# Requesting only k of the third batch ahead of the first expert's w1, with another order for slots 4 to 6

## Chip, cores and metric

One core of a Trainium2 chip. The metric is the device time of one execution in microseconds (us). "Span" is the profiled execution without its fixed start and end, some 1.8 us less than the time. One execution of each kernel is traced; times are medians of several. In the traces PE is TensorE (matmuls), ACT ScalarE, DVE VectorE, POOL GpSimd; PEld is PE's loading of weights; L580 is line 580 of the kernel.

## The reference

Sliding-window attention (8 batches, 8 heads, 576 positions, head size 64; heads 0 to 3 a plain window of 32, heads 4 to 7 a window of 32 steps dilated by 4), then one expert of eight per batch, chosen by the mean of the attention output:

```python
scores = scale * q @ k.T ; scores = where(mask[h], scores, -1e9)
x      = softmax(scores) @ v                       # -> (8, 576, 512)
e      = argmax(x.mean(axis=1) @ w_gate, axis=1)   # one expert per batch
out[b] = gate_w[b] * (relu(x[b] @ w1[e[b]]) @ w2[e[b]])
```

The expert of a batch is known only after all its attention. So w1 (512 x 1024) and w2 (1024 x 512) of a batch can't be requested before that.

## The kernel before

Attention runs in slots, four per batch (two heads each). A slot is: scores (S), exp on ACT (X), mask on VectorE (M), products with v and with ones (A, B), Ln (K, L) and exp (R) for the reciprocal, normalisation (N). Ahead of it k and q are transposed on PE (T) and evacuated by VectorE (D) or ACT (A). Slots 0 to 6 follow a hand-written plan; from slot 7 on a loop mixes slots of batch b+2 with the FFN pieces of batch b. All loads of q, k, v, w1 and w2 are issued by POOL on one queue and cast from fp32 to bf16 on the way.

```python
load_qa(1); load_va(1); load_qb(1); load_vb(1)   # batch 1
load_qa(2)            # k and q of batch 2, heads 4 to 7: 288 KB each
load_va(2)            # its v, 256 KB, and v tail, 64 KB
# ...
def emit_gate(b):
    # gate matmuls on PE, max and index search on VectorE ...
    e_val = nc.values_load(mi[0:1, 0:1].bitcast(I32), engines=[ET.Pool], ...)   # L517
    nc.gpsimd.dma_start(out=w1b[:, 2:4, :], in_=moe_w1[ds(e_val, 1), ...])      # L521, 512 KB
    for a in range(2):
        nc.gpsimd.dma_start(out=w1b[half(a), 0:2, :], in_=moe_w1[...])          # L526, 256 KB each
    if b == 0:
        load_qb(2)            # k and q of heads 0 to 3
        load_w2(e_val, w2b)   # 1024 KB
        load_qa(3); load_vb(2)
    # ... else branch and the loads of batch b + 3
```

In the plan, `T1dk` is the transposes of batch 1's k of heads 4 to 7, `T1dk0D` the evacuation of their first bank (a part of the memory that PE writes to) by VectorE, `C1k` a copy that pairs the heads 0 to 3, `G0` the gate of batch 0, and `F` the first FFN piece: four matmuls of line L580, each reading a different quarter of w1.

The softmax here doesn't subtract the row's maximum and nothing guards it: scores larger than these inputs give would overflow.

## Time and profile before

| | before |
|---|---|
| time, median of 4 runs | 213.13 us (212.65 to 213.38) |
| span of the profiled execution | 210.6 us |
| PE busy | 92% |
| index search of the first gate ends | 23.98 us |
| last piece of the first w1 lands | 34.90 us |
| first FFN matmul (L580) | 35.04 us |

### The profile page before, as it was taken

The numbers are of one execution on the slowest core, as the hardware profiler recorded it, in microseconds if no ns is written. First come the engines' busy times: TensorE is split into PE (matmuls) and PEld (weight loads), VectorE is DVE, ScalarE is ACT, GpSimd is POOL, SyncE is SP. The second block draws the span as 40 slices with busy tenths as digits, with TensorE's granted clock in tenths as the row PEclk, the third lists the DMA queues.
The fourth block names the chain that finished last, engine by engine and source line by source line (L and its number), as shares of the span: only waits on it lengthen the run. The fifth ranks groups of instructions, "written<-read, shape, count | busy, mean of one in ns | idle before, by whom it ended". The sixth has DMA issues, their size and how long they took to land.

```text
span 210.6 us, 7428 instructions
## 1 busy us (share of the span) xinstructions
PE 192.7 (92%) x3130; PEld 140.5 (67%) x3145; DVE 129.2 (61%) x359; ACT 135.7 (64%) x270; POOL 82.5 (39%) x130
## 2 busy tenths in 40 slices
PE   5786775989989999999999999999999999999991
PEld 1565654877658965886578856895588558749741
DVE  5567764686587757775677666875777455325312
ACT  2487695677658876789658865886588656332320
POOL 7977585157460747045442556055104000500000
PEclk9755585899999999999999999999999999999998
DMA  5999999999999999999999999999995993499223
GB/s 73 184 176 193 185 197 210 213 180 202 197 219 246 226 205 195 248 241 209 186 245 251 214 198 250 239 226 210 241 244 98 212 217 134 79 210 230 107 113 111
DMA packets 46416, 41.12 MB, mean 195 GB/s; under 512 B 24880, under 2 KB 34096, under 8 KB 46384
## 3 DMA queue, kind: packets, MB, share of 16 engines
q0 software_dynamic: 38784, 31.20, 96.0%
q1 hardware_dynamic: 7600, 9.46, 13.8%
q8 instruction: 24, 0.39, 0.7%
q14 instruction: 8, 0.07, 0.1%
HBM read 62.41 MB, written 9.44 MB: 341 GB/s over the span
## 4 chain that ended last, share of the span: by engine, by line
PE 79%; DMA 11%; POOL 4%; issue 2%; DVE 1%; ACT 1%; POOLq 0%
PE m L580 31%; PE m L598 26%; PE n L349 8%; PE m L263 7%; DMA qm<-in_q_dram 4%; DMA w1b<-in_moe_w_dram 4%; PE m L613 3%; DMA vm<-in_v_dram 3%; PE ps L284 3%; PE m L510 1%; POOL vm L133 1%; POOL km L118 1%; POOL qm L121 1%; POOL vt L141 0%; ACT qk L271 0%
## 5 line engine op out<-in xcount | busy, mean ns | idle before, releaser
L580 PE MATMUL m<-xt,w1b 128*128 128x288 bf16 x512 | 67.0, 289 | 1.7 <-DMA w1b<-in_moe_w_dram 1.5
L580 PEld LDWEIGHTS <-w1b 128*128 128x128 bf16 x512 | 56.9, 114 | 7.9 <-issue 2.2
L598 PE MATMUL m<-w2b,ht 128*128 128x512 bf16 x241 | 56.9, 379 | 0.9 <-issue 0.2
L583 ACT ACTIVATE ht<-m 128x288 bf16<-128x288 f32 x77 | 31.6, 411 | 21.5 <-PE m L580 17.7
L598 PEld LDWEIGHTS <-ht 128*128 128x128 bf16 x256 | 24.1, 98 | 27.5
L487 DVE SCALAR_TENSOR_TENSOR xt<-n,rd 128x320 bf16<-128x320 f32 (+1 forms) x58 | 29.4, 544 | 11.2 <-ACT rd L460 10.3
L324 DVE TENSOR_TENSOR pt<-pt,mk 128x896 bf16<-128x896 bf16 x32 | 20.0, 625 | 22.1 <-ACT pt L317 22.1
L271 ACT ACTIVATE qk<-m 128x512 bf16<-128x512 bf16 (+1 forms) x28 | 20.8, 742 | 15.6 <-PE m L263 15.2
L317 ACT ACTIVATE pt<-ps 128x896 bf16<-128x896 f32 x32 | 29.0, 906 | 1.4 <-PE ps L284 1.4
L521 POOL DMA_DIRECT2D w1b<-in_moe_w_dram x8 | 5.7, 716 | 61.1 <-PE n L349 32.9
L131 POOL DMA_DIRECT2D vm<-in_v_dram x32 | 24.2, 772 | 10.2 <-DMA w1b<-in_moe_w_dram 3.0
L268 DVE COPY qk<-m 128x640 bf16<-128x640 bf16 (+1 forms) x28 | 22.3, 797 | 6.6 <-PE m L263 6.6
L585 DVE TENSOR_SCALAR ht<-m 128x288 bf16<-128x288 f32 x51 | 22.6, 455 | 4.7 <-PE m L580 3.8
L605 DVE TENSOR_SCALAR osb<-m,gbc 128x512 f32<-128x512 f32 x16 | 12.0, 747 | 17.7 <-PE m L598 17.7
L460 ACT ACTIVATE rd<-lnd 128x576 f32<-128x576 f32 x32 | 21.9, 684 | 1.0
L455 ACT ACTIVATE lnd<-n 128x256 f32<-128x256 f32 (+1 forms) x58 | 20.6, 406 | 1.7 <-PE n L349 1.6
L349 PEld LDWEIGHTS <-vm 64*64 64x64 bf16 x896 | 14.8, 114 | 9.2 <-SPq L410 2.8
L349 PE MATMUL n<-pt,vm 64*64 64x64 bf16 (+2 forms) x816 | 19.0, 198 | 1.6 <-DVE pt L324 1.2
L349 PE MATMUL n<-pt,ones 64*64 64x128 bf16 (+3 forms) x262 | 17.4, 251 | 0.0
L603 ACT ACTIVATE osb<-m,gbc 128x512 f32<-128x512 f32 x16 | 10.9, 682 | 8.7 <-PE m L598 8.7
L284 PEld LDWEIGHTS <-qk 64*64 64x64 bf16 x608 | 14.2, 116 | 2.8 <-issue 1.7
L284 PE MATMUL ps<-qk 64*64 64x96 bf16 (+3 forms) x608 | 14.8, 211 | 1.3 <-ACT pt L317 1.1
(72 smaller groups left out, 196.3 us busy)
## 6 DMA issues: line engine op xcount, KB each, us to landing
w2b<-in_moe_w_dram POOLq DMA_DIRECT2D x8, 1024.0 KB, 11.1
out_dram<-osb SPq DMA_DIRECT2D x32, 256.0 KB, 6.7
km<-in_k_dram POOLq DMA_DIRECT2D x16, 288.0 KB, 10.9
qm<-in_q_dram POOLq DMA_DIRECT2D x16, 288.0 KB, 11.3
w1b<-in_moe_w_dram POOLq DMA_DIRECT2D x8, 512.0 KB, 7.4
w1b<-in_moe_w_dram POOLq DMA_DIRECT2D x16, 256.0 KB, 8.3
vm<-in_v_dram POOLq DMA_DIRECT2D x8, 256.0 KB, 9.9
vm<-in_v_dram POOLq DMA_DIRECT2D x32, 64.0 KB, 7.9
```

Source lines behind the costliest of these rows:

```text
L131: nc.gpsimd.dma_start(out=t[:, h], in_=v[b, h, 0:512, :].rearrange("(c p) d -> p c d", p=P))
L268: nc.vector.tensor_copy(out=ev[x][0], in_=ev[x][1])
L271: nc.scalar.activation(out=ev[x][0], in_=ev[x][1], func=AF.Copy)
L284: nc.tensor.matmul(ps[half(e), a, o : o + rhs.free_size()], lhsT=lhsT, rhs=rhs, start=True, stop=True, skip_group_check=True)
L317: nc.scalar.activation(out=pt[:], in_=s["ps"][:, :, 0:NP], func=AF.Exp, scale=0.125)
L349: x = nc.tensor.matmul(oo, lhsT=lhsT, rhs=rhs, start=start, stop=True, skip_group_check=True)
L460: nc.scalar.activation(out=rd[:], in_=s["lnd", n][:], func=AF.Exp, scale=-1.0)
L487: nc.vector.scalar_tensor_tensor(out=o, in0=a0, scalar=1.0, in1=a1, op0=ALU.mult, op1=ALU.mult, accum_out=s["pool"][:, w, c : c + 1],)
L580: nc.tensor.matmul(hm, lhsT=w[:, fc % 4, :], rhs=s["xt"][:, c, cols], start=(c == 0), stop=(c == 3))
L583: nc.scalar.activation(out=o, in_=hm, func=AF.Relu)
L585: nc.vector.tensor_scalar_max(out=o, in0=hm, scalar1=0.0)
L598: nc.tensor.matmul(om, lhsT=s["ht"][:, fc, r * P : (r + 1) * P], rhs=s["w2"][:, fc, :], start=(fc == 0), stop=(fc == 7))
```

## The change

Intent: less should stand ahead of w1 in the load queue, and slots 4 to 6 should end earlier, so that the first FFN matmul starts earlier.

```diff
-    load_qa(2)
-    load_va(2)
+    load_tiles(2)
+    load_1(2, GO[0], "k")
@@ emit_gate, b == 0, after the three w1 requests
+            load_1(2, GO[0], "q")
+            load_va(2)
             load_qb(2)
             load_w2(e_val, w2b)
@@ plan, slots 4 to 6
-  ... T1dk L3 C1k R3 T1dk0A
-  N3 G0 T1dq T1dk1D T1dq0A T1pk T1dq1D C1q T1pk0A S4 T1pk1D T1pq X4 M4 S5 T1pq1D T1pq0A A4 X5 B4 K4 M5 L4 S6 R4
-  A5 X6 B5 K5 L5 N4 S7 M6 R5 A6 X7 N5 B6 K6 L6 M7 F R6 ...
+  ... T1dk L3 T1dk0D R3
+  T1dk1A N3 T1dq T1dq0A C1k G0 T1dq1A T1pk C1q S4 T1pk0D X4 T1pk1D T1pq T1pq0A S5 M4 T1pq1D X5 A4 K4 B4 L4 S6 M5 R4
+  A5 X6 B5 K5 L5 N4 S7 M6 R5 A6 X7 N5 B6 K6 L6 F M7 R6 ...
```

More of the change, by code (lines that the diff above doesn't have):

```diff
@@ L692 @@
         T0dk:7 MB T0dk0D T0dk1A T0dq D2 T0dq0A T0dq1D S0 C0k X0 T0pk M0 S1 T0pk1A C0q X1 T0pk0D T0pq T0pq0A M1 A0 T0pq1D
-        B0 K0 S2 L0 R0 A1 X2 N0 B1 K1 S3 L1 M2 R1 A2 X3 N1 B2 K2 L2 M3 R2 A3 N2 B3 K3 T1dk L3 C1k R3 T1dk0A
-        N3 G0 T1dq T1dk1D T1dq0A T1pk T1dq1D C1q T1pk0A S4 T1pk1D T1pq X4 M4 S5 T1pq1D T1pq0A A4 X5 B4 K4 M5 L4 S6 R4
-        A5 X6 B5 K5 L5 N4 S7 M6 R5 A6 X7 N5 B6 K6 L6 M7 F R6 T2dk T2dk0D T2dk1A N6
+        B0 K0 S2 L0 R0 A1 X2 N0 B1 K1 S3 L1 M2 R1 A2 X3 N1 B2 K2 L2 M3 R2 A3 N2 B3 K3 T1dk L3 T1dk0D R3
+        T1dk1A N3 T1dq T1dq0A C1k G0 T1dq1A T1pk C1q S4 T1pk0D X4 T1pk1D T1pq T1pq0A S5 M4 T1pq1D X5 A4 K4 B4 L4 S6 M5 R4
+        A5 X6 B5 K5 L5 N4 S7 M6 R5 A6 X7 N5 B6 K6 L6 F M7 R6 T2dk T2dk0D T2dk1A N6
     """
```

## The prediction

> **What bounds the kernel now.** I read the page first (PE 92% busy, and the slices show it nearly full from slice 8 of 40 on), then the chain that ended last in order of time. Its columns are start us, length us, and what:
>
> ```profile
> 14.97 8.24 DMA qm<-in_q_dram
> ...
> 26.18 0.59 POOL w1b L526
> 26.77 8.13 DMA w1b<-in_moe_w_dram
> 34.90 0.14 issue
> 35.04 1.12 PE m L580 x4
> 36.16 2.05 PE m L263 x18
> ```
>
> Before 34.90 us the chain runs through the load queue (POOL issues and DMA); from 35.04 us it is PE almost without a break to the end at 206.3. The joint is the first FFN matmul (L580): it waits for the last piece of the first expert's w1. The waits of PE after 35 us, longest first (total us, times, longest us), confirm it:
>
> ```profile
> PE m L580 <- DMA w1b<-in_moe_w_dram: 1.5, 1, 1.5
> PE m L263 <- DVE kx L247: 1.0, 1, 1.0
> PE m L510 <- ACT ht L583: 0.5, 1, 0.5
> ```
>
> So the kernel is a start-up of 35 us and some 171 us of dense PE. A change to loads is worth what it moves the start of the first L580; later loads are worth nothing while they land in time.
>
> The timeline of instructions shows what PE did before that start (start us, us, engine, line, ..., idle before and its releaser):
>
> ```profile
> 33.23 0.30 PE L349 MATMUL n<-pt,ones 64*64 64x128 bf16 x4
> 35.04 1.12 PE L580 MATMUL m<-xt,w1b 128*128 128x288 bf16 x4 [1.51 <-DMA w1b<-in_moe_w_dram]
> ```
>
> PE finished slot 6's last attention product at 33.53 and stood 1.51 us. That is all that an earlier w1 alone can give. To give more, the work of slots 4 to 6 must also end earlier: the second half of the change.
>
> The timeline of POOL, which issues all loads, around the first w1:
>
> ```profile
> 19.97 0.55 POOL L121 DMA_DIRECT2D km<-in_k_dram  x1
> 21.21 0.54 POOL L121 DMA_DIRECT2D qm<-in_q_dram  x1 [0.69 <-DMA km<-in_k_dram]
> 23.49 0.75 POOL L133 DMA_DIRECT2D vm<-in_v_dram  x1 [1.74 <-DMA qm<-in_q_dram]
> 24.23 0.63 POOL L141 DMA_DIRECT2D vt<-in_v_dram  x1
> 25.48 0.70 POOL L521 DMA_DIRECT2D w1b<-in_moe_w_dram  x1 [0.62 <-issue]
> 26.18 1.21 POOL L526 DMA_DIRECT2D w1b<-in_moe_w_dram  x2
> ```
>
> The first four are the third batch's k, q, v and v tail. Counting back, each waiting issue waits for the load eight issues earlier (vm at 23.49 for the qm of 14.97, which landed at 23.21): eight loads are in flight at most. I took the time to landing of single issues from the DMA view, one narrow window per issue (KB, us to landing); four of them are
>
> ```profile
> km<-in_k_dram POOLq DMA_DIRECT2D x1, 288.0 KB, 6.3
> qm<-in_q_dram POOLq DMA_DIRECT2D x1, 288.0 KB, 6.5
> vm<-in_v_dram POOLq DMA_DIRECT2D x1, 256.0 KB, 5.5
> w1b<-in_moe_w_dram POOLq DMA_DIRECT2D x1, 512.0 KB, 6.6
> ```
>
> Added to the issue times these land at 26.3, 27.7, 29.0 and 32.1 us, the v tail at 29.4 (24.23 + 5.2), and the last w1 piece at 34.9: in order of issue, at the rate of the queue (288 KB in 1.4 us is 206 GB/s). w1's last piece is late because 608 KB stand between it and k.
>
> **What the Trainium skill says.** "DMA: Bandwidth & Descriptors", section "Two DMAs through the same engine are not ordered", says that descriptors of one queue of one engine start in order but are pipelined. The landings above agree: they come in order, so what is requested ahead is paid for by what comes behind. The same page, section "Bandwidth", gives about 358 GB/s as HBM's share of one core. The page of this trace has 62.41 MB read for 31.20 MB that the load queue wrote, and 341 GB/s over the span with the stores; the loads run near that figure, so w1 comes earlier only if fewer bytes go first. "TensorE: Matmul & The Clock Gate", section "Part 1: The HAM clock gate", says that the clock is half unless PE was busy through a free-running window of about 3.4 us. The stretches of one us agree (PE, PEld, DVE, ACT, POOL busy, then clock, DMA, GB/s):
>
> ```profile
> 28.00:29.00 1.00, 0.90 (x50) 0.57 (x43) 0.65 (x2) 0.94 (x2) 1.00 (x3) 0.84 1.22 206
> 31.00:32.00 1.00, 0.39 (x18) 0.26 (x17) 1.00 (x3) 0.97 (x4) 0.00 (x0) 0.86 1.15 211
> 38.00:39.00 1.00, 0.92 (x6) 0.54 (x5) 1.00 (x4) 0.77 (x1) 0.62 (x1) 0.72 1.01 205
> ```
>
> From the mean clocks it steps up at about 28.3, down at 31.7 and up at 38.6, distances of 3.4 and 6.9 us. The first FFN matmuls run 3.5 us at half clock.
>
> **The change, part by part.**
>
> *Requests.* Taken from ahead of w1: q (288 KB), v (256 KB), v tail (64 KB), 608 KB. In landings: 29.4 - 26.3 = 3.1 us. They are now issued right after w1, ahead of q and k of the other half. Nothing is added; the sum of bytes down to that other half's q is the same. By landings alone w1 would end at 34.9 - 3.1 = 31.8.
>
> But w1 cannot be asked for before the gate knows the expert. The index search ends at 23.98 on VectorE, and POOL issues w1 at 25.48, 1.50 us later; in the next two batches, where no load is being issued just then, the distance is 1.31 (47.03 to 48.34) and 1.24 (68.55 to 69.79). So the issue moves from 25.48 to about 25.25. At the end of the kernel, with the load queue empty, w1 issued at 180.20 needs 5.1 us to its first piece, and the last piece, issued about 181.5, 5.8: some 7.1 us from first issue to last landing. 25.25 + 7.1 = 32.4. This is later than 31.8, so the queue runs dry for some 0.6 us between k and w1, and w1 lands at about 32.4: 2.5 us earlier.
>
> *Does the gate itself move?* The new order puts the gate's matmuls behind the q transposes of batch 1's first half (T1dq), and one VectorE evacuation (0.82) ahead of slot 3's normalisation. PE stands from 21.6 to 23.14 now, waiting for the pooled sum (22.91 + 0.16 on VectorE), so T1dq (1.14 at half clock) fits into that hole: its q was requested at 12.39 and landed at 17.8. The evacuation fits in between 21.25 (five transposes done) and 22.07; the normalisation starts at 22.03 now, since it waits for the reciprocal on ACT (21.31 + 0.68). VectorE's pair copy (C1k, 0.46) now fills the wait for the gate's matmuls (23.07 to 23.5). The gate therefore keeps its time within 0.1 us.
>
> *Slots 4 to 6.* Now: T1dq 23.45, T1pk 24.39, scores of slot 4 at 25.48, its exp at 26.14, then ACT is nearly full until 34.28. New: T1dq is done by 22.7; T1pk starts after the gate and the pair copy at about 23.6, ends at 24.75 (1.14); scores of slot 4 from 24.75 (0.61), exp at about 25.4. That is 0.75 us earlier. From there to the last Ln of slot 6 the ACT work is the same in both orders (four exps, one transposed half, Lns and reciprocals), and batch 1's first k half of T1pk (0.77) goes from ACT to VectorE ahead of it, so the 0.75 is carried through: slot 6's products end on PE at about 33.53 - 0.75 = 32.8.
>
> *Sum.* The first L580 starts at the later of 32.4 (w1, + 0.14) and 32.8 (PE), so 32.8 instead of 35.04: 2.2 us. After it everything is PE work that moves along, if its loads are there: q of batch 2 lands behind w1 at 32.4 + 1.4 = 33.8 and is wanted at 32.8 + 2.2 (first piece and k transposes at half clock) = 35.0. k of the other half landed at 36.1, at most about 36.7 with the dry 0.6 us, and its pair copy moves from 40.17 to 38.0. First w2 landed at 42.5 and is wanted at 50.2 - 2.2 = 48. No load becomes a bound. 213.24 - 2.2 = 211.0 us, 1.0% less.
>
> **The rivals.** (1) *Only PE's wait goes*: the order of slots 4 to 6 gains nothing because ACT, not PE, sets it (ACT busy 0.9 or more of most us from 26 to 33), or VectorE, which now has two T1pk evacuations (0.8 + 0.7) ahead of slot 4's mask, delays it. Against it: the mask waits for ACT anyway until 26.3, about when they end. Gain then 1.5 us, 211.7. (2) *A new wait behind w1*: q of batch 2 later than 35.0, or k for the pair copy. The margins are about 1.2 us each by the working above, so a miss would cost a few tenths; 211.5. (3) *The clock*: PE now starts its dense stretch at another place in the 3.4 us windows. It met one at the best moment now (35.04, edge at about 35.15). With the edges where they are it would either count the window from 31.7 as busy and be at full clock at 35.15 (gain up to 0.6 more), or stay at half until 38.6, 5.8 us instead of 3.5, and lose 2.3 / 2 = 1.1 of the gain. Free-running windows move between runs of both kernels, so the medians should average this; it makes the range, 210.2 to 212.2. (4) *The gate slips* by T1dq (1.1 us) if that waits for a bank or its load: w1 at 33.5, gain 1.4, 211.8.
>
> **Range and chances.** Centre 211.0. The clock gives about +1.1 or -0.6, rivals 1, 2 and 4 up to +0.8 each, hardly together: 209.9 to 212.4. More than 2% would be a gain of 4.3 us; neither w1 (2.5) nor PE's end of slot 6 (0.75) can reach it, so 4%. A loss of 2% would need a wait of over 6 us that no load shows: 1%.
>
> **What would show it.** Right: w1's first issue near 25.25 with the index search near 24.0; its last landing near 32.4; PE's idle ahead of the first L580 down from 1.51 to a few tenths; exp of slot 4 near 25.4; the first L580 near 32.8; and from there to the end 171 us as now. Wrong: an index search a us later (rival 4); the exp of slot 4 still near 26.1 (rival 1); a DMA wait in front of batch 2's transposes or copies (rival 2); or a length from first L580 to the end that differs from 171 by about one us, with the clock's steps elsewhere (rival 3).

## More of the kernel before

The page gives the rate at which DMA moved bytes in 40 slices of 5.3 us. It stays between 176 and 251 GB/s (stores included) from the second slice to the thirtieth, without a gap:

```profile
GB/s 73 184 176 193 185 197 210 213 180 202 197 219 246 226 205 195 248 241 209 186 245 251 214 198 250 239 226 210 241 244 98 212 217 134 79 210 230 107 113 111
```

As milestones for "how far is PE" I use the last matmuls of each batch's FFN (L613). First and last, from the timeline of PE in the kernel before:

```profile
60.14 1.06 PE L613 MATMUL m<-w2b,ht 128*64 128x256 bf16 x16
205.18 1.06 PE L613 MATMUL m<-w2b,ht 128*64 128x256 bf16 x16
```

And the issue of the last v tail, from the timeline of POOL, as a milestone for the load stream:

```profile
144.75 0.62 POOL L139 DMA_DIRECT2D vt<-in_v_dram  x1 [0.55 <-DMA qm<-in_q_dram]
```

## The result and the profile after

213.26 us median (213.18 to 213.55, 4 runs) against 213.13; ratio 1.0012, 95% interval 0.9991 to 1.0032: no change.

The start of the dense stretch, from the timeline of PE in the changed kernel (its L582 is L580 of before):

```profile
32.54 0.30 PE L349 MATMUL n<-pt,ones 64*64 64x128 bf16 x4
34.48 1.12 PE L582 MATMUL m<-xt,w1b 128*128 128x288 bf16 x4 [1.64 <-DMA w1b<-in_moe_w_dram]
```

Slot 6 ends at 32.84 (32.54 + 0.30), as predicted (32.8), but w1 is not there: PE stands 1.64 us, more than before. The first FFN matmul comes 0.56 us earlier, not 2.2. The step of the chain that releases it:

```profile
27.23 7.11 DMA w1b<-in_moe_w_dram
```

w1's last piece lands at 34.34, not at 32.4. POOL and the stream around it, from the timeline of POOL and from stretches of one us (busy shares of PE, PEld, DVE, ACT and POOL, then clock, DMA share, GB/s). The 5.51 us ahead of the first w1 request are POOL's wait for the gate; the releaser named there is the trace's inference:

```profile
19.88 0.55 POOL L121 DMA_DIRECT2D km<-in_k_dram  x1
25.95 0.70 POOL L521 DMA_DIRECT2D w1b<-in_moe_w_dram  x1 [5.51 <-DVE qk L268]
26.64 1.21 POOL L526 DMA_DIRECT2D w1b<-in_moe_w_dram  x2
27.82 0.59 POOL L121 DMA_DIRECT2D qm<-in_q_dram  x1
```

```profile
24.00:25.00 1.00, 1.00 (x9) 0.84 (x9) 0.94 (x6) 0.31 (x1) 0.00 (x0) 1.00 0.78 133
25.00:26.00 1.00, 1.00 (x27) 0.92 (x26) 1.00 (x2) 0.31 (x1) 0.05 (x1) 1.00 0.11 21
26.00:27.00 1.00, 1.00 (x27) 0.80 (x26) 0.60 (x2) 1.00 (x2) 1.00 (x2) 1.00 0.06 16
27.00:28.00 1.00, 0.76 (x42) 0.46 (x32) 0.91 (x2) 1.00 (x2) 1.00 (x3) 1.00 0.46 33
...
40.00:41.00 1.00, 1.00 (x8) 0.72 (x6) 0.58 (x3) 0.34 (x1) 0.31 (x2) 0.71 1.08 218
```

In the kernel before the four rates from 24 to 28 us were 208, 206, 186 and 181 GB/s; here they sum to 203 instead of 781. Against 800, four us at 200 GB/s, about 3.0 us of the load stream are lost. After this the stream does not catch up. The same milestone as before, from the timeline of POOL:

```profile
147.94 0.62 POOL L139 DMA_DIRECT2D vt<-in_v_dram  x1 [0.65 <-DMA qm<-in_q_dram]
```

It is 3.2 us later: what was lost ahead of w1 is still missing 120 us on. One late load shows what this does: k of the last batch, heads 4 to 7. Its issue by POOL, its time to landing (last number, from the DMA view) and its transposes on PE, in the kernel before and then in the changed one:

```profile
126.04 0.56 POOL L121 DMA_DIRECT2D km<-in_k_dram  x1
km<-in_k_dram POOLq DMA_DIRECT2D x1, 288.0 KB, 11.4
140.74 0.67 PE L263 MATMUL m<-identb,km 128*128 128x128 bf16 x9
```

```profile
129.22 0.57 POOL L121 DMA_DIRECT2D km<-in_k_dram  x1
km<-in_k_dram POOLq DMA_DIRECT2D x1, 288.0 KB, 12.3
141.55 0.67 PE L263 MATMUL m<-identb,km 128*128 128x128 bf16 x9
```

This k landed at 137.4 and was used at 140.74, 3.3 us later; now it lands at 141.5 and is used at once. From these transposes to the last milestone below it is 64.4 us in both kernels, so their start, 0.81 us later, sets the end. PE's milestones (L615 is L613 of before):

```profile
60.59 1.06 PE L615 MATMUL m<-w2b,ht 128*64 128x256 bf16 x16
206.00 1.06 PE L615 MATMUL m<-w2b,ht 128*64 128x256 bf16 x16
```

The 0.56 us won at the first FFN matmul are 0.45 lost by the first milestone and 0.82 at the last. A first loss is the clock: from the mean clock of its stretch it stepped to full at about 40.6, 6.1 us after the first FFN matmul, against 38.6 and 3.5 us before; 2.6 us more at half speed are about 1.3 us. The other 0.4 us go around a pause of PE near 64.1 us for which the trace names no wait.

A caution for reading: the clock column says 1.00 from 18 to 30 us here, yet the nine transposes of T1dk took 1.14 us in both kernels, and in the one before the column said 0.50. "TensorE: Matmul & The Clock Gate", section "Part 1: The HAM clock gate", warns that clock events of a trace were seen to be unreliable; this trace agrees. I take the clock from durations where the two differ.

Absolute times also hide something. In this execution T1dk started at 20.93 us, against 20.46, because the clock fell to half earlier (the transposes of batch 0's first k took 1.14 us instead of 0.68). I therefore count from T1dk's start or from the end of the index search. The search ended 3.52 us after T1dk's start in both: the gate did not slip. Counted so, slot 6 ended 11.9 us after T1dk's start, where the prediction had 12.3 (32.8 - 20.46): that its 32.8 was met is in part luck, a late start and a quicker run that cancel. And w1 came 9.9 us after the search instead of 10.9.

### The profile page after: what moved, and what is told of

The parts are those of the page before. It is cut to its first block, busy times and chain, and to the rows that moved or that the text cites. A ratio compares the mean times of both kernels' runs of the same rounds, so it can differ in the third digit from the quotient of the medians.

```text
span 211.4 us, 7442 instructions
## 1 busy us (share of the span) xinstructions
PE 196.2 (93%) x3145; PEld 141.6 (67%) x3145; DVE 129.3 (61%) x359; ACT 135.4 (64%) x270; POOL 82.4 (39%) x130
## 3 DMA queue, kind: packets, MB, share of 16 engines
q0 software_dynamic: 38784, 31.20, 96.0%
HBM read 62.41 MB, written 9.44 MB: 340 GB/s over the span
## 4 chain that ended last, share of the span: by engine, by line
PE 85%; DMA 6%; DVE 3%; ACT 2%; issue 2%; POOL 1%; POOLq 0%; SPq 0%
PE m L582 32%; PE m L600 27%; PE n L349 9%; PE m L263 8%; DMA w1b<-in_moe_w_dram 3%; PE m L615 3%; PE ps L284 3%; DMA qm<-in_q_dram 2%; PE m L510 1%; PE n L263 1%; DVE xt L487 1%; ACT pt L317 1%; ACT rd L460 1%; PE m L349 1%; DVE pt L324 1%
## 5 line engine op out<-in xcount | busy, mean ns | idle before, releaser
L582 PE MATMUL m<-xt,w1b 128*128 128x288 bf16 x512 | 68.2, 292 | 1.6 <-DMA w1b<-in_moe_w_dram 1.6
L582 PEld LDWEIGHTS <-w1b 128*128 128x128 bf16 x512 | 57.2, 115 | 8.7 <-issue 2.2
L600 PE MATMUL m<-w2b,ht 128*128 128x512 bf16 x256 | 57.8, 379 | 0.0
L271 ACT ACTIVATE qk<-m 128x512 bf16<-128x512 bf16 (+1 forms) x27 | 20.0, 740 | 15.3 <-PE m L263 14.9
L268 DVE COPY qk<-m 128x640 bf16<-128x640 bf16 (+1 forms) x29 | 23.1, 798 | 7.0 <-PE m L263 7.0
L605 ACT ACTIVATE osb<-m,gbc 128x512 f32<-128x512 f32 x16 | 10.9, 682 | 8.7 <-PE m L600 8.7
## 6 DMA issues: line engine op xcount, KB each, us to landing
w2b<-in_moe_w_dram POOLq DMA_DIRECT2D x8, 1024.0 KB, 12.1
```

The lines of the kernel that those rows point to most:

```text
L268: nc.vector.tensor_copy(out=ev[x][0], in_=ev[x][1])
L582: nc.tensor.matmul(hm, lhsT=w[:, fc % 4, :], rhs=s["xt"][:, c, cols], start=(c == 0), stop=(c == 3))
L600: nc.tensor.matmul(om, lhsT=s["ht"][:, fc, r * P : (r + 1) * P], rhs=s["w2"][:, fc, :], start=(fc == 0), stop=(fc == 7))
```

## The experiments

Three theories came out of this, the third only after the run after_hot. **1, hidden bytes:** the 608 KB moved behind w1 used to flow while POOL waited for the gate and for w1's first bytes, so w1 gains only about 1 us by their absence, and the stream runs dry. **2, clock:** what PE gained at the first FFN matmul went in a later clock step. **3, given back:** the load stream has almost no slack against PE, so the dry 3 us come back later as waits or as less room to run ahead. Their rivals stand with each run. The first four ran on one chip, and so did each later group.

**One half of the change alone.** `req_only` has the new requests with the old plan, `order_only` the old requests with the new plan:

```diff
 req_only:   (new requests)
-        ... T1dk L3 T1dk0D R3 ...      # new plan
+        ... T1dk L3 C1k R3 T1dk0A ...  # old plan, whole
 order_only: (old requests, new plan, whole)
```

> The new requests with the old order of slots 4 to 6. Theory 1 (the moved 608 KB were mostly hidden: they flowed while POOL waited for the gate and for the first bytes of w1): the last w1 piece lands about 9.9 us after the index search ends, against 10.9 before, so the first L580 starts about 1.0 us earlier measured from the search; slot 6's last product still ends about 9.5 us after the search. Time within 0.6 us of before. Rival (the requests are worth the 2.5 us of the prediction and the new order eats it): first L580 about 1.5 us earlier, limited by slot 6, and 211.7 us.

Measured 212.83 us, ratio 0.9979 (0.9951 to 1.0006). w1 10.1 us after the search, first FFN matmul 13.8 us after T1dk's start (14.6 before). As theory 1 has it. Its trace has a wait of PE for k at 118.62 us, 1.3 us long, that the kernel before does not have.

> The old requests with the new order. Theory 1: slot 6 ends about 0.7 us earlier measured from the first T1dk transpose, w1 lands about 10.9 us after the search, so the first L580 stays where it was in before (near 35.0 us) and PE idles about 2.2 us ahead of it; time within 0.4 us of before. Rival (the new order delays the gate by about 0.5 us): the search ends about 4.0 us after the start of T1dk instead of 3.5, and the time is 0.5 us longer.

Measured 213.38 us, ratio 1.0006 (0.9977 to 1.0034). Slot 6 ends 12.4 us after T1dk's start (13.1 before), the search 3.52: the new order works and does not delay the gate. But w1 landed 9.9 us after the search, not 10.9, and the first FFN matmul came 13.6 us after T1dk's start: that part of the expectation missed. With the old requests w1's delay turned out to vary: 10.9, 9.9, 11.2 and 12.1 us in four traces (before, this one, and two below); with k alone ahead it was 9.8 to 10.1 in all six traces. So one trace of the kernel before was a thin base for theory 1's "one us".

**The clock.** Dummy matmuls in PE's idle time, so that the clock steps earlier (`after_hot` on the changed kernel, `before_hot` on the one before):

```diff
-        ... R5 A6 X7 N5 B6 K6 L6 F ...
+        ... R5 A6:1 X7 N5 B6 K6 L6 F:4 ...    # n dummies into the bank used next
```

> The changed kernel with one dummy matmul ahead of slot 6's products and four ahead of the first L580, in PE's idle time. Theory 2 (what the earlier first L580 gained was lost again because the clock stepped to full 6.2 us after it in the changed kernel's profile and 3.5 us after it in that of before): the step comes 0 to 3 us after the first L580, the time is near 211.3, 1.5 to 2.5 us less than the changed kernel. Rival (the clock is not the cause; PE after the first L580 is bound by evacuations or loads): the time stays near 213.2 even where the step comes earlier.

Measured 213.49 us, ratio 1.0011 (0.9983 to 1.0039). The expected time missed. The clock did step at the first FFN matmul, and PE's first milestone came 2.67 us earlier than in the changed kernel; at the last one only 0.29 us were left (of both, 1.13 us are an earlier start of T1dk in this execution: counted from it, 1.54 us won had become 0.84 lost; L617 is L615):

```profile
57.92 1.06 PE L617 MATMUL m<-w2b,ht 128*64 128x256 bf16 x16
205.71 1.06 PE L617 MATMUL m<-w2b,ht 128*64 128x256 bf16 x16
```

The timeline of PE says where it went: waits for q and k of later batches.

```profile
35.31 0.68 PE L263 MATMUL m<-identb,qm 128*128 128x128 bf16 x9 [0.88 <-DMA qm<-in_q_dram]
72.29 0.68 PE L263 MATMUL m<-identb,km 128*128 128x128 bf16 x9 [0.63 <-DMA km<-in_k_dram]
118.57 0.68 PE L263 MATMUL m<-identb,km 128*128 128x128 bf16 x9 [1.28 <-DMA km<-in_k_dram]
```

This is where theory 3 came from.

> The kernel before with the same five dummy matmuls. Theory 2: near 211.8, and the difference to after_hot is what the change is worth once the clock is out of it, 0.5 to 1.0 us by theory 1. If the difference is 2 us, theory 1 falls; if it is nothing, w1's earlier landing is worth nothing even with the clock taken out.

Measured 213.25 us, ratio 0.9985 (0.9949 to 1.0021); two of six executions at 211.6 and 211.9, four at 213.2 to 213.8. The expectation (211.8) missed, and so did its reading of the difference. Why only two executions gained is open: only one of those was traced.

**Less to load.** Batch 1 uses the w2 of batch 0, so 1024 KB or about 5 us of the stream fall away and PE does the same work; the result is wrong. On `after_hot` and on the kernel before, later also on the changed kernel without dummies:

```diff
-        w2b = wp.tile([P, 8, DM], BF16, name="w2b", tag="w2b")
+        w2b = st[0]["w2"] if b == 1 else wp.tile([P, 8, DM], BF16, name="w2b", tag="w2b")
@@
-            load_w2(e_val, w2b)
+            if b != 1:
+                load_w2(e_val, w2b)
```

> after_hot with one load left out: batch 1 uses the w2 of batch 0 (1024 KB, about 5 us of the load stream; the result is wrong on purpose, every matmul stays). Theory 3 (what PE wins early is given back later, because the load stream runs full from the start to about 157 us and has almost no slack: the 3 us in which it ran dry ahead of w1 come back as waits of PE for k and q near 60, 70, 118 and 140 us): those waits, 2.8 us in after_hot, vanish and the time is near 210.5, 2.5 to 3 us less than after_hot. Rival (PE's later waits have another cause, or the clock): the time stays near 213.

Measured 210.8 us, ratio 0.9886 (0.9857 to 0.9915), 2.7 us less than `after_hot`; no wait of PE for a load from 40 us on. The value expected, within 0.3 us.

> The kernel before with the same load left out (wrong result on purpose). Theory 3: its stream had no dry stretch and PE did not wait for k or q in its profile, so the time falls little, by 0 to 1.0 us (only in runs whose clock let PE run ahead). Rival: the kernel before is bound by loads as much as after_hot, then it falls by 2 us or more too.

Measured 213.37 us, ratio 1.0009 (0.9972 to 1.0046). Nothing gained: the kernel before is not held by its loads. Its trace had w1 at 12.1 us after the search:

```profile
36.44 1.12 PE L581 MATMUL m<-xt,w1b 128*128 128x288 bf16 x4 [2.46 <-DMA w1b<-in_moe_w_dram]
```

> The changed kernel, without dummy matmuls, with batch 1 using the w2 of batch 0 (1024 KB less to load; wrong result on purpose). It parts what loads and what the clock take. Theory 3 (loads give it back): without the waits for k and q the time falls by 0.5 to 1.5 us against the 213.3 of the changed kernel, and the rest down to the 210.8 of after_hot_less is the clock's (theory 2), 0.7 to 2 us. Rival to theory 2 (dummy matmuls do nothing): after_less is at 210.8 like after_hot_less. Rival to theory 3: after_less is at 213.3, all is the clock.

Measured 211.7 us, ratio 0.9918 (0.9877 to 0.9958): 1.6 us less than the changed kernel's 213.26 (by the ratios, 1.0012 and 0.9918, 2.0; the two ran in different groups). That is read as what the loads took. The dummies of `after_hot_less` bring another 0.9 us (by the ratios 0.0032 of 213, or 0.7): the clock's part, at the lower end of what theory 2 expected, but the two intervals overlap, so it is not clear of noise. The loads' part is clear of it; its size is not exact. The two traced executions differ by only 0.38 us from T1dk's start to the last batch's k transposes, but this k has 3.1 us to spare in after_less (landed 137.3, used 140.35) and none in the changed kernel.

So with loads out of the way the change is worth 211.7 against 213.37, 1.7 us (the ratios, 0.9918 and 1.0009, give 1.9). This is close to the 2.2 predicted, in part by luck: w1 was not as early as predicted, but the kernel before had it later (12.1 us after the search in before_less) than in the one trace that the prediction rests on. The load stream takes the gain away.

**More or less requested ahead**, all with the new plan:

```diff
 q_ahead:     k and q ahead of w1           +    load_1(2, GO[0], "q")   # ahead, instead of behind
 v_ahead:     k, v and v tail ahead, q behind +  load_va(2)
 none_ahead:  nothing of batch 2 ahead      -    load_1(2, GO[0], "k")   # now behind w1
```

> The changed kernel with q (288 KB) put back ahead of w1; v and its tail stay behind. Theory 1: the load stream is dry for about 1.9 us instead of 3.3 between 24 and 29 us, yet w1 lands as late after the index search as in the changed kernel (9.7 to 10.1 us), because q flows in the time in which w1's first bytes are not there yet. Theory 3: later loads land about 1.4 us earlier than in the changed kernel, the time is 0 to 1 us less than it. Rival (bytes ahead of w1 count one for one): w1 lands 1.4 us later after the search, 11.3.

Measured 212.2 us, ratio 0.9969 (0.994 to 0.9998). w1 9.3 us after the search although 288 KB more stood ahead of it (9.9 in its second trace, below). The rival's 11.3 falls. The stream was dry for 1.3 us, less than the 1.9 expected.

> The changed kernel with k too behind w1, so that nothing of the third batch is requested ahead. Theory 1: the stream runs dry for about 4.5 us, w1 lands 9.6 to 9.9 us after the search, no earlier than in the changed kernel. Theory 3: later loads land about 1.4 us later still, and the time rises by 1 to 2 us over the changed kernel, with waits of PE for k, q or v. Rival (only w1 and the clock count): the time stays within 0.5 us.

Measured 214.48 us, ratio 1.0067 (1.0038 to 1.0096), 1.2 us over the changed kernel. w1 9.7 us after the search: k's absence gained it nothing. Waits of PE for q at 36.59 (0.91 us) and for k at 142.19 (0.53).

Then the changed kernel, q_ahead and v_ahead on one chip:

> The changed kernel again. Theories 2 and 3: 213.0 to 213.6, ratio to before 0.997 to 1.002; last w1 9.7 to 10.1 us after the search; if its clock steps within 4 us of the first L580, its trace has a wait of PE for k of 0.5 us or more between 60 and 145 us; if it steps 5 us or later, none.

Measured 213.23 us, ratio 1.0002 (0.9953 to 1.0052), w1 9.8 us after the search. The clock stepped 5.4 us after the first FFN matmul, and the wait was there all the same, so the dividing line that I had drawn was wrong; the wait itself is theory 3's:

```profile
141.13 0.68 PE L263 MATMUL m<-identb,km 128*128 128x128 bf16 x9 [0.63 <-DMA km<-in_k_dram]
```

In the first trace of the changed kernel the same transposes ran at 141.55 without a wait, since k had landed just then (141.5): what the late clock cost there, the wait would have cost otherwise. PE can't pass this point before its k lands, 141.1 to 141.5 us in the changed kernel's two traces and in after_hot, however early it starts.

> q_ahead again, beside the changed kernel. Theory 3: 0.6 to 1.4 us less than after_again. Rival (the earlier gain was the chip's or the clock's luck): within 0.3 us of it.

Measured 211.67 us, ratio 0.9926 (0.9881 to 0.9971), 1.6 us less than after_again: a little more than expected. From T1dk's start to the last milestone the traces differ by 1.44 us; 0.58 of it was there at the first milestone, so the wait for k (0.63) and the stream are not the whole of it. But its k of the last batch landed at 139.6, just as PE came (139.63): 1.5 us later, as in after_again, it would have taken that back. So loads are a limit in q_ahead too.

> The changed kernel with v and its tail (320 KB) put back ahead of w1 and q (288 KB) behind. Theory 1 and 3: as q_ahead, since only the amount counts: last w1 9.3 to 10.0 us after the search, dry for 1.3 to 2.0 us, time 0.6 to 1.4 us less than after_again. Rival (v is what delayed w1 in the kernel before): last w1 10.5 us or more after the search and no gain over after_again.

Measured 211.88 us, ratio 0.9934 (0.9886 to 0.9983), 1.35 us less than after_again, as theory 3 has it. But w1 landed 11.0 us after the search and the first FFN matmul 14.8 us after T1dk's start: here the rival is right as well, v ahead seems to delay w1: with v and its tail right ahead of it w1 came after 9.9 to 12.1 us in five traces, without them after 9.3 to 10.1 in ten (the kernels with w1 in more pieces aside). The gain came all the same. Its k of the last batch had 2.0 us to spare (landed 138.7, used 140.68). So by the medians a fuller stream was worth more here than an earlier w1. The traced execution, at 212.31 one of the slower ones, does not show the gain: from T1dk's start to the last milestone it took 185.4 us, as long as after_again's.

The series in one table. "Dry" is the shortfall against 200 GB/s from 24 to 28 us (22 to 28 for none_ahead) divided by 200; the last v tail is the milestone of the load stream.

| ahead of w1 | kernel | dry, us | last v tail issued, us | fastest run, us | ratio to before |
|---|---|---|---|---|---|
| 0 KB | none_ahead | 4.3 | 149.29 | 213.82 | 1.0067 |
| 288 KB, k | changed kernel, twice | 3.0, 2.6 | 147.94, 147.44 | 212.47 | 1.0012, 1.0002 |
| 576 KB, k and q | q_ahead, twice | 1.3, 1.0 | 146.21, 146.03 | 211.19 | 0.9969, 0.9926 |
| 608 KB, k, v, v tail | v_ahead | 0.9 | 145.58 | 211.41 | 0.9934 |
| 896 KB, all | order_only | 0.4 | 145.73 | 212.92 | 1.0006 |
| 896 KB, all | kernel before | 0.1 | 144.75 | 212.11 (of 48) | 1 |

From 0 to 576 KB each 288 KB put ahead bring the stream about 1.6 us forward (means of the two traces where there are two) and the fastest run 1.3 us down. Between 608 and 896 KB this ends: the stream gains no more, and the kernel is as slow as the one before, which has the same requests. A late w1 (10.9 to 12.1 us after the search in three of four traces) is the likely cause, but order_only's own trace had it at 9.9, so this end of the series is argued, not shown. Loads are not the reason in its trace: k of the last batch had 2.9 us to spare. The milestone itself is not the stream's alone: before_less has it at 146.35 with 1024 KB less to load, so differences of some 1.6 us between two single traces should not be read from it alone.

**Tries at a faster kernel.** `q_ahead_hot` is q_ahead with the five dummies. `q_split` is q_ahead with w1 of batch 0 loaded as two halves of its columns, `q_split_hot` that with three dummies:

```diff
+        for f0, f1 in ((0, F // 2), (F // 2, F)) if b == 0 else ((0, F),):
-                out=w1b[:, 2:4, :], in_=moe_w1[ds(e_val, 1), 256:512, :]...
+                out=w1b[:, 2:4, f0:f1], in_=moe_w1[ds(e_val, 1), 256:512, f0:f1]...
```

> q_ahead (212.2) with the five dummy matmuls. Theory 3: its load stream is 1.4 us ahead of the changed kernel's, so that much of an earlier clock step can be kept: 211.0 to 211.8, a correct kernel faster than both. Rival: it stays at 212.2 since loads bind again (waits for k or q in its trace) or the dummies do nothing.

Measured 212.17 us, ratio 0.9956 (0.9911 to 1.0): no better than q_ahead, as the rival said; PE waits for k at 140.50 (0.19 us), so loads bind again, barely.

> q_ahead with the first w1 loaded in two halves by columns, first the half that the first L580 pieces use. The first half lands about 2.5 us before the whole did, so the first L580 no longer waits for w1 but for slot 6 (about 32.8 after a search at 24.0). q_ahead's profile had only 0.5 us of PE idle left there, so theory: 0.3 to 0.8 us less than q_ahead, 211.6. Rival: the six smaller issues slow the load stream (rows of 2 KB instead of 4) and the time stays or rises.

Measured 213.83 us, ratio 1.0023 (0.9981 to 1.0066). The first FFN matmul did start at 32.43 us, but the next three of its piece stood 2.55 us until 35.41, just after the last of the six w1 pieces landed (35.27), though they need the first half alone. Why they wait for the second half is open. That the first goes and the next waits would fit a dependence kept by the first and last address of a piece, since the second half of row blocks 0 and 1, as one range, takes in block 1's first half but not block 0's; this was not tried. The expected gain missed.

> q_split with one dummy ahead of slot 6's products and two ahead of the first L580. Theories 2 and 3: the earliest start and an earlier clock step, bound then by loads (waits for k or q in its trace): 210.8 to 211.8. Rival: no better than q_split.

Measured 214.28 us, ratio 1.0044 (1.0006 to 1.0083), with the same wait.

The version to keep is q_ahead: correct, and faster than the kernel before in both of its groups, by 0.3% and 0.7% (both intervals end below 1). Beside the changed kernel it ran once, and all its six executions were faster than all six of that.

## Why the prediction was wrong, step by step

- **What bounds the kernel: half right.** The first FFN matmul is the joint, and its start matters. That "later loads are worth nothing while they land in time" held for the kernel before (before_less gains nothing) but left out how little time there is: 3.3 us at the last batch's k (2.9 in order_only and 3.1 in before_less, but 0.4 in before_hot).
- **Gate and order of slots 4 to 6: right in kind.** Search 3.52 us after T1dk's start in both kernels; slot 6 at 32.84 (predicted 32.8, met in part by luck, as said above).
- **w1 at 32.4: wrong, it was 34.34.** Three terms. The search came 0.47 us late with T1dk (clock at the start, not the change). Search to issue stayed 1.50 us instead of 1.27. First issue to last landing was 8.4 us instead of 7.1; the 7.1 took the time of w1's second piece at the end of the kernel (5.8) for that of the third (about 6.4, which makes 7.7). What makes up the rest was not tried. In the traced execution the late w1 alone took 1.64 of the 2.2 us at the first FFN matmul (34.48 instead of 32.84).
- **"The queue runs dry for some 0.6 us": wrong, 3.0 us.** I took the landing of k as the end of the data ahead of w1. In the changed kernel k still landed at 26.4 (19.88 + 6.5), as predicted, but the rate had fallen to 21 GB/s by 25 us, 1.4 us before that landing. And w1's own data did not flow before about 28 us (33 GB/s from 27 to 28), 2 us after its issue.
- **"No load becomes a bound": wrong, and this is the step that failed the sum.** I checked the first loads behind w1, one by one, and found slack of over a us for each. I did not check the stream as a whole: it runs full until about 157 us, so 3 us lost at 25 us are missing behind, and k of the last batch landed 4.1 us later (141.5 for 137.4). It had 3.3 us to spare, and a PE that is 2.2 us ahead leaves 1.1. With 1024 KB less to load the changed kernel is 1.6 us faster, the kernel before not at all.
- **"The loads run near that figure" of 358 GB/s: wrong, but nothing rests on it alone.** The 341 GB/s are a mean over the whole span. At the stream's 206 GB/s written, with twice as much read (62.41 MB for 31.20), the reads come to some 410 GB/s, an estimate from these numbers: 358 was no limit here. And that fewer bytes ahead make w1 earlier did not hold: 0, 288 and 576 KB gave 9.7, 9.8 to 10.1 and 9.3 to 9.9 us after the search.
- **Rival 2, "a miss would cost a few tenths", had the right mechanism and too small a size;** it looked for the wait at batch 2, and it is found as far as batch 7's k.
- **Rival 3, the clock, was right in the traced execution** (6.1 us at half instead of 3.5). Taking it out with dummies gained under 1 us with less to load, not clear of noise, and nothing without.

## What to carry to other kernels

When requests move behind a transfer that can't be issued yet, ask what the queue does meanwhile: bytes that flow while nothing else could cost w1 nothing here, and taking them away left a hole that the full stream of this kernel did not close. Check the slack of a saturated stream over the whole kernel, down to the last loads that PE wants, not load by load near the edit. The best amount ahead lay in the middle here (576 to 608 KB of 0 to 896). The landing and the use of such a load show in one trace which side waits for the other.

## What the Trainium skill lacked or had wrong

- "DMA: Bandwidth & Descriptors", section "Anatomy of one DMA", fits a load from POOL as about 2.0 us plus bytes over 436 GB/s. For the first 512 KB of w1, with the stream dry, this gives, as an estimate, 3.2 us by the bytes written and 4.4 by the fp32 bytes read; the changed kernel's took 5.3 us, with w1's other two pieces in flight beside it. What a cast in the load does to its rate is not said; the stream here wrote about 205 GB/s.
- No page says how far w1's landing scatters when other loads stand right ahead of it: 9.9 to 12.1 us after the search with the old requests, 9.7 to 10.1 with k alone or nothing ahead.
